# Normalizing rows ahead of an MLP and splitting the last output sums: a polynomial attention and Fourier mixing kernel on one core

## The chip, the cores and the metric

The kernel runs on one core of one Trainium2 chip. The metric is the device time of one execution in microseconds (us). A core has five engines with a queue of instructions each: TensorE (PE, matrix products; PEld are its weight loads), VectorE (DVE), ScalarE (ACT), GpSimd (POOL) and SyncE (SP, which here issues transfers). They run side by side and wait for each other by semaphores. TensorE writes its products to PSUM, which has 8 banks of 512 f32 columns by 128 partitions; the other data stands in SBUF.

## The reference: what is computed

Four batches, 4 heads, 1088 tokens, head size 32. First an attention with polynomial features, without softmax:

```
a, b  = S1 x, S2 x                     (8 values each per token, for q and k)
phi   = outer(a, b)                    (64 features)
kv    = sum over tokens of phi(k) v    z = sum over tokens of phi(k)
x     = (phi(q) kv) / (phi(q) z + 1e-6)          -> [batch, 1088, 128]
```

Then a mixing layer and an MLP:

```
u   = x + real(FFT over tokens and over the 128 features of x)
un  = (u - mean(u)) / sqrt(var(u) + 1e-6)        (per token)
out = u + relu(un @ w1) @ w2                     (128 -> 512 -> 128)
```

## The kernel before, in words

The whole order is written out by hand in one table (lines 28 to 79). A word such as `UB,A,-1,0,2` names a step, the engine that carries it out (P, V, A, G for POOL, S), the PSUM bank (or -1) and the step's arguments, mostly batch and group. Each engine carries out its own words in the table's order; the framework adds the waits. In what follows a step is named with its arguments: UB 0,2 is batch 0, group 2.

The 1088 tokens of a batch are cut into groups 0 and 1 of 512 (four blocks of 128) and group 2 of 64. For each batch:

- **Attention.** LQ, LK, LV load. QT, KT transpose on VectorE. QA, QB (lines 394 and 398) project q into PSUM, QE copies one factor out, and QM (VectorE, line 414) or QF and QG (ScalarE and POOL, lines 420 and 424) multiply the two. KP, KE and KM (POOL, line 365) do the same for k, KV (line 371) sums over tokens, KZ (line 389) copies kv and z out. ND and NN (lines 429 and 436) are the denominator and the numerator; DT, DE, RC, BT make the reciprocals, XM (line 466) gives x in bf16.
- **Mixing.** FD (line 478) is the transform over features, PE (line 490) copies it out, TD (line 496) is the transform over tokens, TE and CX (lines 513 and 516) copy it out. AN and XN make reversed copies for group 1.
- **u and its statistics, batches 0 to 2.** UU (line 584) makes rows of u in PSUM, token by token, US (line 593) copies them to SBUF in f32, UB (line 531) casts them to bf16, TP (line 542) transposes them with TensorE, UE (line 549) copies the transposed block out. BS (line 535) takes the row statistics, SD (line 573) the square root of the variance for all nine blocks of a batch at once, RS (line 581) its reciprocal.
- **u, batch 3.** UT (line 520) makes u transposed and centred straight away, UQ squares it, VR sums the squares, VT transposes the sums, and then come SD and RS. UU and US follow late, for the output sum alone.
- **MLP.** w1 is centred over its rows ahead of time (CM, CE), so that u need not be. M1 (line 599) multiplies by w1, RL (line 614) applies the relu, M2 (line 625) multiplies by w2. A factor 1/std per token passes through relu and both products, so the kernel multiplies by it only at the end.
- **Output.** For batches 0, 2 and 3, FS (line 659, instructions of line 664) computes product times 1/std plus u, in blocks of 128 columns on VectorE. For batch 1, groups 0 and 1, FM (line 642) multiplies on VectorE and FA (line 653) adds on POOL. ST (line 669) stores a group in two halves (rho 0 and 1), from SP but for three of batch 3's stores, which ScalarE's queue issues. The output tile `ot` has one buffer for group 0 and one for group 1, so a batch's sums wait for the stores of the batch before.

Buffers that differ by batch (us, ub, uT, X, AB, rs, sd) are taken in turns of two; hT, the relu's output, in turns of three.

Of the kernel before, what the change touches and what calls it, by code (L numbers as in the profile page):

```python
# [28 lines left out]
INIT0,V,-1 LS,A,-1,1 INIT,G,-1 LQ,S,-1,0,0 LS,S,-1,0 SX,V,-1 QT,V,-1,0,0 LQ,S,-1,0,1 QT,V,-1,0,2 LK,S,-1,0,0
QT,V,-1,0,1 LK,S,-1,0,1 LQ,S,-1,1,1 KT,V,-1,0,0 SQ,A,-1 SA,A,-1,1 INI2,G,-1 SA,G,-1,0 SC,G,-1 WARM,P,0,0 WARM,P,1,1  # L30
WARM,P,2,2 WARM,P,3,3 WARM,P,4,4 WARM,P,5,5 WARM,P,6,6 WARM,P,7,7 QA,P,0,0,0 QE,A,-1,0,0,1 QE,A,-1,0,0,0 QB,P,4,0,0
QA,P,0,0,1 QM,V,-1,0,0,1 KT,V,-1,0,1 QF,A,-1,0,0,0 KP,P,4,0 QE,A,-1,0,1,0 QE,A,-1,0,1,1 QT,V,-1,1,1 QA,P,0,1,1
QE,A,-1,1,1,0 KE,V,-1,0 QB,P,4,0,1 LV,S,-1,0,0 SB,S,-1,1 LQ,S,-1,1,0 SB,S,-1,2 LV,S,-1,0,1 QE,A,-1,1,1,1 QT,V,-1,1,0
QT,V,-1,1,2 QA,P,0,1,0 VP,A,-1,0 QM,V,-1,0,1,0 QM,V,-1,0,1,1 QG,G,-1,0,0,0 KM,G,-1,0,0 SB,S,-1,3 LK,S,-1,1,1
KT,V,-1,1,1 KV,P,4,0,0 KM,G,-1,0,1 SB,S,-1,4 LK,S,-1,1,0 QE,A,-1,1,0,1 QE,A,-1,1,0,0 QB,P,0,1,0 KT,V,-1,1,0 KP,P,5,1
QF,A,-1,1,0,0 QF,A,-1,1,0,1 KV,P,-1,0,1 KE,V,-1,1 KZ,A,-1,0,2 KZ,A,-1,0,1 QB,P,0,1,1 SB,S,-1,5 LK,S,-1,2,0 KT,V,-1,2,0
SB,S,-1,6 LV,S,-1,1,1 KZ,A,-1,0,0 KZ,A,-1,0,3 SB,S,-1,7 LK,S,-1,2,1 KM,G,-1,1,0 KM,G,-1,1,1 ND,P,7,0,0 QM,V,-1,1,1,1
SB,S,-1,8 LV,S,-1,1,0 KT,V,-1,2,1 ND,P,4,0,1 DT,V,-1,0,0 VP,A,-1,1 KW,P,5,1,0 DE,V,-1,0,0 DT,V,-1,0,1 QM,V,-1,1,1,0
SB,S,-1,9 LB,S,-1 SB,S,-1,10 LK,S,-1,3,1 SB,S,-1,11 LQ,S,-1,2,1 QG,G,-1,1,0,1 NN,P,1,0,1 SB,S,-1,12 LQ,S,-1,2,0
DE,A,-1,0,1 RC,V,-1,0,1 RC,V,-1,0,0 SB,S,-1,13 LV,S,-1,2,1 KP,P,6,2 QG,G,-1,1,0,0 BT,V,-1,0,1 KW,P,-1,1,1 QT,V,-1,2,0  # L40
QT,V,-1,2,2 XM,V,-1,0,1 QB,P,0,2,0 KE,V,-1,2 NN,P,6,0,0 SB,S,-1,14 LK,S,-1,3,0 SB,S,-1,15 LC,S,-1,2 SB,S,-1,16
LV,S,-1,2,0 KZ,A,-1,1,0 KZ,A,-1,1,3 KZ,A,-1,1,1 KZ,A,-1,1,2 ND,P,5,1,0 SB,S,-1,17 LC,S,-1,0 SB,S,-1,18 LQ,S,-1,3,0
SB,S,-1,19 LC,S,-1,1 SB,S,-1,20 LW,S,-1,2 SB,S,-1,21 LQ,S,-1,3,1 QT,V,-1,2,1 BT,V,-1,0,0 QF,A,-1,2,0,1 ND,P,4,1,1
XM,V,-1,0,0 QF,A,-1,2,0,0 QA,P,0,2,1 DT,V,-1,1,0 FD,P,6,0 KM,G,-1,2,0 DT,V,-1,1,1 QE,A,-1,2,1,0 QE,A,-1,2,1,1
NN,P,4,1,0 DE,A,-1,1,1 PE,A,-1,0,1 PE,A,-1,0,0 DE,V,-1,1,0 RC,V,-1,1,0 KT,V,-1,3,1 QA,P,0,2,0 QE,A,-1,2,0,1
QE,A,-1,2,0,0 BT,V,-1,1,0 TD,P,6,0 TE,A,-1,0 CX,A,-1,0,0 VP,G,-1,2 XM,V,-1,1,0 RC,V,-1,1,1 KM,G,-1,2,1 KT,V,-1,3,0
NN,P,4,1,1 CX,A,-1,0,2 CW,A,-1,2 CX,A,-1,0,1 BT,V,-1,1,1 CX,V,-1,0,3 KP,P,2,3 XM,V,-1,1,1 KV,P,0,2,0 XN,G,-1,0
QG,G,-1,2,0,1 QB,P,4,2,1 KE,V,-1,3 FD,P,2,1 UU,P,1,0,0 SB,S,-1,22 LV,S,-1,3,1 QF,A,-1,2,1,1 AN,A,-1,0 QG,G,-1,2,0,0
SB,S,-1,23 LW,S,-1,1 SB,S,-1,24 LV,S,-1,3,0 PE,A,-1,1,1 VP,G,-1,3 QT,V,-1,3,0 QT,V,-1,3,2 QM,V,-1,2,1,0 PE,V,-1,1,0
QA,P,4,3,0 UU,P,2,0,1 KV,P,-1,2,1 US,V,-1,0,1 US,A,-1,0,0 QG,G,-1,2,1,1 UB,G,-1,0,1 KM,G,-1,3,0 QE,A,-1,3,0,1  # L50
QE,A,-1,3,0,0 QT,V,-1,3,1 BS,V,-1,0,0 KZ,V,-1,2,0 CW,A,-1,1 KZ,V,-1,2,2 QB,P,4,3,0 UU,P,3,0,2 QF,A,-1,3,0,1
US,A,-1,0,2 XN,A,-1,1 TD,P,1,1 TE,A,-1,1 CX,A,-1,1,2 CX,A,-1,1,0 CX,A,-1,1,3 KZ,V,-1,2,1 KZ,V,-1,2,3 QG,G,-1,3,0,1
KM,G,-1,3,1 ND,P,0,2,0 QM,V,-1,3,0,0 BS,V,-1,0,1 CX,V,-1,1,1 UB,A,-1,0,0 UB,A,-1,0,2 ND,P,3,2,1 DT,V,-1,2,0
DE,A,-1,2,0 DT,V,-1,2,1 QA,P,4,3,1 CM,P,1 CE,V,-1 DE,A,-1,2,1 RC,V,-1,2,1 RC,V,-1,2,0 UU,P,2,1,2 QE,A,-1,3,1,0
QE,A,-1,3,1,1 TP,P,0,0,0 KV,P,3,3,0 TP,P,1,0,1 UE,A,-1,0,1 UE,A,-1,0,0 BT,V,-1,2,1 US,V,-1,1,2 UB,G,-1,1,2 AN,G,-1,1
NN,P,4,2,1 NN,P,6,2,0 UU,P,2,1,0 M1,P,0,0,1,1 BT,V,-1,2,0 BS,V,-1,0,2 XM,V,-1,2,0 XM,V,-1,2,1 KV,P,-1,3,1 QB,P,4,3,1
US,V,-1,1,0 UB,G,-1,1,0 SD,A,-1,0 RL,A,-1,0,1,1 QF,A,-1,3,1,1 FD,P,0,2 QM,V,-1,3,1,0 TP,P,2,1,2 UU,P,4,1,1
M1,P,5,0,0,0 PE,A,-1,2,0 BS,V,-1,1,0 PE,V,-1,2,1 US,V,-1,1,1 BS,V,-1,1,2 RS,V,-1,0 KZ,A,-1,3,3 UE,A,-1,1,2 KZ,A,-1,3,2
KZ,A,-1,3,0 KZ,A,-1,3,1 TP,P,7,1,0 RL,A,-1,0,0,0 M1,P,0,0,0,1 QG,G,-1,3,1,1 UB,G,-1,1,1 XN,G,-1,2 RL,A,-1,0,0,1
UE,V,-1,1,0 BS,V,-1,1,1 TD,P,2,2 TP,P,4,0,2 M1,P,6,1,0,0 UE,A,-1,0,2 M1,P,0,0,1,0 M1,P,4,0,2,0 M2,P,5,0,0 TE,V,-1,2  # L60
RL,V,-1,0,2,0 RL,A,-1,1,0,0 CX,A,-1,2,1 RL,A,-1,0,1,0 FS,V,-1,0,0,0 TP,P,4,1,1 UE,A,-1,1,1 CX,V,-1,2,0 ND,P,6,3,0
ND,P,7,3,1 CX,A,-1,2,3 DT,V,-1,3,0 DT,V,-1,3,1 ST,S,-1,0,0,0 M1,P,0,1,0,1 DE,A,-1,3,0 FS,V,-1,0,0,1 SD,A,-1,1
M1,P,4,1,2,0 M2,P,6,0,2 DE,A,-1,3,1 RS,V,-1,1 RC,V,-1,3,1 CX,A,-1,2,2 FS,V,-1,0,2,0 M2,P,7,0,1 M1,P,2,1,1,0
RL,A,-1,1,0,1 RL,A,-1,1,2,0 RC,V,-1,3,0 FS,V,-1,0,1,0 FS,V,-1,0,1,1 BT,V,-1,3,0 RL,A,-1,1,1,0 UU,P,5,2,0 M1,P,0,1,1,1
AN,G,-1,2 US,A,-1,2,0 UB,A,-1,2,0 ST,S,-1,0,0,1 BT,V,-1,3,1 M2,P,6,1,0 NN,P,2,3,0 NN,P,4,3,1 RL,A,-1,1,1,1 FM,V,-1,1,0
UU,P,7,2,1 FA,G,-1,1,0 XM,V,-1,3,0 M2,P,0,1,1 XM,V,-1,3,1 US,A,-1,2,1 UB,A,-1,2,1 TP,P,6,2,0 FD,P,3,3 BS,V,-1,2,1
UU,P,1,2,2 UE,A,-1,2,0 FM,V,-1,1,1 ST,S,-1,0,2,0 M2,P,2,1,2 ST,S,-1,0,1,0 ST,S,-1,0,1,1 US,V,-1,2,2 BS,V,-1,2,0
PE,A,-1,3,0 PE,A,-1,3,1 M1,P,5,2,0,0 TP,P,7,2,1 RL,V,-1,2,0,0 FA,G,-1,1,1 UB,G,-1,2,2 M1,P,0,2,0,1 UE,A,-1,2,1
RL,A,-1,2,0,1 TD,P,3,3 TE,A,-1,3 CX,A,-1,3,1 ST,S,-1,1,0,0 CX,A,-1,3,2 ST,S,-1,1,0,1 CX,A,-1,3,3 TP,P,7,2,2
M1,P,5,2,1,0 M1,P,0,2,1,1 UE,V,-1,2,2 FS,V,-1,1,2,0 BS,V,-1,2,2 SD,A,-1,2 M2,P,7,2,0 ST,S,-1,1,1,1 ST,S,-1,1,1,0  # L70
RL,A,-1,2,1,0 CX,V,-1,3,0 UT,P,3,3,2 UT,P,2,3,1 UE,A,-1,3,1 UT,P,4,3,0 RL,V,-1,2,1,1 M1,P,6,2,2,0 M2,P,5,2,1
UE,A,-1,3,0 M1,P,0,3,0,1 UQ,A,-1,3,2 RL,A,-1,2,2,0 ST,S,-1,1,2,0 UQ,A,-1,3,1 UQ,A,-1,3,0 RS,V,-1,2 FS,V,-1,2,0,0
FS,V,-1,2,0,1 ST,S,-1,2,0,0 FS,V,-1,2,1,0 UE,V,-1,3,2 M1,P,6,3,0,0 UU,P,2,3,0 FS,V,-1,2,1,1 M2,P,3,2,2 US,V,-1,3,0
RL,A,-1,3,0,1 VR,P,4,3 M1,P,0,3,1,1 RL,A,-1,3,0,0 FS,V,-1,2,2,0 M1,P,2,3,1,0 M2,P,6,3,0 ST,S,-1,2,0,1 ST,S,-1,2,1,0
AN,G,-1,3 XN,G,-1,3 UU,P,5,3,1 M1,P,7,3,2,0 VT,V,-1,3 SD,A,-1,3 RL,A,-1,3,1,0 RL,V,-1,3,1,1 M2,P,2,3,1 ST,S,-1,2,1,1
ST,S,-1,2,2,1 US,A,-1,3,1 RL,A,-1,3,2,0 UU,P,4,3,2 ST,S,-1,2,2,0 RS,V,-1,3 FS,V,-1,3,0,0 FS,V,-1,3,0,1 M2,P,5,3,2
FS,V,-1,3,1,0 ST,S,-1,3,0,0 US,A,-1,3,2 ST,A,-1,3,0,1 ST,S,-1,3,1,0 FS,V,-1,3,2,0 FS,V,-1,3,1,1 ST,A,-1,3,2,0
ST,A,-1,3,2,1 ST,S,-1,3,1,1
"""


# [60 lines left out]
class Steps:  # L142
# [389 lines left out]
        n, m, c = (128, 4, 4 * g) if g < 2 else (64, 1, 8)  # L532
        self.copy(e, self.ub[b % 2][0:n, c : c + m, :], self.us[b % 2][0:n, c : c + m, :])

    def BS(self, e, bk, b, g):
# [4 lines left out]
        self.whole.add(b)  # L540
# [81 lines left out]
        else:  # L622
            self.nc.vector.tensor_scalar(out=out, in0=in_, scalar1=0.0, scalar2=None, op0=MAX)

    def M2(self, e, bk, b, g):
# [30 lines left out]
        self.eng(e).tensor_tensor(out=self._oo(b, g), in0=_ap(self.tm[g], 0, n, 0, dims),  # L656
                                  in1=_ap(self.us[b % 2], 0, n, 512 * g, dims), op=ADD)

    def FS(self, e, bk, b, g, rho):
        n = 128 if g < 2 else 64  # L660
        for f in range(2 if g < 2 else 1):
            i = 2 * f + rho
            o = 0 if g == 2 else 256 * rho + 128 * (1 - f if g == 0 else f)
            self.nc.vector.scalar_tensor_tensor(  # L664
                out=self.o2[b % 2][:, :] if g == 2 else self.ot[g][:, o : o + 128], in0=self.bank(("m2", b, g), 0, n, 128 * i, [[1, 128]]),
                scalar=self.rs[b % 2][0:n, 4 * g + i : 4 * g + i + 1], in1=self.us[b % 2][0:n, 4 * g + i, :],
                op0=MULT, op1=ADD)
# [61 lines left out]
```

## Time and profile before

| what | value |
|---|---|
| median of three executions | 81.86 us (81.79 to 82.59) |
| profiled execution | 81.78 us, span 79.9 us |
| TensorE busy | 69.3 us (87% of the span) |
| VectorE busy | 61.4 us (77%) |
| ScalarE busy | 55.0 us (69%) |
| GpSimd busy | 42.2 us (53%) |
| chain that ended last | PE 53%, ACT 22%, DVE 7%, DMA 5% |
| last matrix product starts | 74.43 us and just after (4 weight loads, M2 3,2) |
| last output sum ends | 75.89 us |

The span runs from the first to the last instruction that the profiler saw. Matrix products are pipelined: each is shown with its latency (0.22 us for 128 columns in bf16), while the next starts 0.055 us later, so a step's length on TensorE is read from one step's start to the next one's. The profile's groups give the count of a kind of instruction, its busy time and the mean of one; the chain follows from the last instruction back to what released it.

### The profile page before, as it was taken

The page shows a single profiled execution, that of the slowest core. Times are in us where ns is not written, and L with a number is a line of the kernel's source. Part 1 is how long each engine was busy: PE and PEld are TensorE (multiplying, and loading weights), DVE is VectorE, ACT ScalarE, POOL GpSimd, SP SyncE. Part 2 cuts the span into 40 slices and gives each one's busy share as a digit, 9 for nine tenths or more (in the row PEclk, how much of TensorE's full clock was granted, in tenths as well). Part 3 has the DMA queues.
Part 4 walks back from the last instruction along what each step waited for, and adds up shares of the span by engine and source line. Part 5 has one row for each costly group of instructions (what it writes and reads, how often), then busy time and mean ns, then how long its engine had stood idle before and what let it go on. Part 6 is the DMA issues. An engine that isn't in the chain of part 4 may idle for free.

```text
span 79.9 us, 3447 instructions
## 1 busy us (share of the span) xinstructions
PE 69.3 (87%) x1457; PEld 41.4 (52%) x1462; DVE 61.4 (77%) x144; ACT 55.0 (69%) x114; POOL 42.2 (53%) x60
## 2 busy tenths in 40 slices
PE   3949799798899999799999999999999998999400
...
DVE  1055757949999996978999989769998868899800
ACT  2412657859209579487999669998998789997300
POOL 6840338939999999995999167101142705000000
...
GB/s 24 188 315 369 278 335 285 259 245 325 288 285 300 309 232 231 12 0 8 4 8 0 8 0 8 0 0 66 83 143 41 91 131 25 36 187 57 66 211 6
DMA packets 8659, 10.90 MB, mean 136 GB/s; under 512 B 1092, under 2 KB 5956, under 8 KB 8644
## 3 DMA queue, kind: packets, MB, share of 16 engines
...
## 4 chain that ended last, share of the span: by engine, by line
PE 53%; ACT 22%; DVE 7%; DMA 5%; issue 4%; POOL 3%; SPq 1%; DVEq 0%; ACTq 0%
PE banks L235 53%; ACT hT L621 10%; DMA qin<-in_q_dram 5%; ACT aS L222 4%; POOL kp L367 3%; ACT AB L222 2%; DVE ot L664 1%; ACT us L222 1%; ACT vpad L222 1%; DVE ab L363 1%; DVE qp L416 1%; DVE X L469 1%; SPq L232 1%; ACT hE L621 1%; DVE kT L343 1%
## 5 line engine op out<-in xcount | busy, mean ns | idle before, releaser
L367 POOL TENSOR_TENSOR kp<-ab 128x1152 f32<-128x1152 f32 x8 | 17.3, 2173 | 3.1 <-DVE ab L363 3.1
L222 ACT COPY aS<-banks 128x576 f32<-128x576 f32 (+1 forms) x16 | 9.0, 616 | 6.8 <-PE banks L235 6.7
L621 ACT ACTIVATE hT<-banks 128x1024 bf16<-128x1024 f32 x13 | 13.2, 1039 | 0.5 <-PE banks L235 0.4
L426 POOL TENSOR_TENSOR qp<-bS,aS 128x576 f32<-128x576 f32 (+1 forms) x8 | 10.9, 1376 | 4.6 <-ACT bS L222 4.6
L235 PE MATMUL banks<-qp,kvz 64*32 64x256 f32 (+3 forms) x192 | 9.7, 398 | 0.4 <-ACT kvz L222 0.3
L235 PE MATMUL banks<-uT,w1c 128*128 128x512 bf16 (+1 forms) x44 | 9.1, 312 | 0.4
L235 PE MATMUL banks<-w2b,hT 128*128 128x128 bf16 x128 | 8.5, 219 | 0.1
L235 PEld LDWEIGHTS banks<-vpad,kp 128*32 128x32 f32 (+1 forms) x504 | 6.6, 113 | 3.6 <-POOL kp L367 2.4
L235 PE MATMUL banks<-qT,sab 32*64 32x288 f32 x128 | 7.1, 501 | 1.5 <-DVE qT L348 1.3
L664 DVE SCALAR_TENSOR_TENSOR ot<-banks,rs,us 128x128 f32<-128x128 f32 x24 | 7.0, 342 | 1.5 <-PE banks L235 0.7
L235 PEld LDWEIGHTS <-hT 128*128 128x128 bf16 x128 | 7.5, 98 | 1.1 <-ACT hT L621 0.4
L235 PE MATMUL banks<-vpad,kp 128*32 128x34 f32 (+1 forms) x504 | 7.5, 202 | 0.7 <-ACT vpad L222 0.3
L235 PE MATMUL banks<-qU,sab 32*64 32x256 f32 x128 | 6.8, 496 | 0.9 <-DVE X L469 0.6
L416 DVE TENSOR_TENSOR qp<-banks,aS 128x512 f32<-128x512 f32 (+1 forms) x8 | 5.5, 697 | 2.4 <-PE banks L235 2.3
L235 PE MATMUL banks<-cb,X 128*128 128x256 bf16 (+1 forms) x56 | 7.2, 250 | 0.0
L222 ACT COPY bS<-banks 128x576 f32<-128x576 f32 (+1 forms) x8 | 4.8, 630 | 3.0 <-PE banks L235 1.9
L235 PEld LDWEIGHTS <-X 128*128 128x128 bf16 x56 | 5.2, 98 | 2.6 <-issue 1.7
L226 POOL COPY ABn<-AB 128x512 bf16<-128x512 bf16 x3 | 1.8, 610 | 8.5 <-ACT AB L222 8.5
L538 DVE BATCH_NORM_STATS2 st<-us 128x6 f32<-128x256 f32 (+1 forms) x15 | 5.7, 410 | 0.1
L469 DVE TENSOR_TENSOR X<-banks,rb 128x512 bf16<-128x512 f32 (+1 forms) x8 | 5.5, 714 | 0.2
L464 DVE STREAM_TRANSPOSE rb<-rc 128x512 f32<-128x512 f32 (+1 forms) x8 | 5.6, 716 | 0.0
L343 DVE STREAM_TRANSPOSE kT<-kin 128x544 f32<-128x544 f32 x8 | 5.6, 712 | 0.0
...
## 6 DMA issues: line engine op xcount, KB each, us to landing
...
```

The costliest lines, as they stand in the source:

```text
L222: self.nc.scalar.copy(out, in_)
L226: self.nc.gpsimd.tensor_copy(out, in_)
L235: self.nc.tensor.matmul(out, l, r, start=start, stop=stop)
L343: self.nc.vector.transpose(self.kT[b % 2][:, 576 * i : 576 * i + 544], self.kin[b % 2][:, 544 * i : 544 * i + 544])
L367: self.eng(e).tensor_tensor(out=_ap(self.kp[b % 2], 0, 128, 1152 * p, [[64, 18], [8, 8], [1, 8]]), in0=_ap(a, 0, 128, 288 * p, [[16, 18], ...
L416: self.nc.vector.tensor_tensor(out=self.qp[b % 2][:, 2 * u : 2 * u + 2, o : o + n], in0=self.bank(("qb", b, r), off=1024 * u, dims=[[512, ...
L426: self.eng(e).tensor_tensor(out=self.qp[b % 2][:, 2 * u : 2 * u + 2, o : o + n], in0=self.bS[u][:, :, 0:n], in1=self.aS[b % 2][:, 2 * u : ...
L464: self.nc.vector.transpose(self.rb[r][:, :, 0 : 32 * n], _ap(self.rc[r], 0, 128, 0, [[1, 2], [2, n], [0, 32]]))
L469: self.nc.vector.tensor_tensor(out=out, in0=self.bank(("nn", b, r), dims=[[512, 2], [1, n]]), in1=self.rb[r][:, :, 0:n], op=MULT)
L538: self.nc.vector.bn_stats(self.st[b % 2][0:n, 2 * g + i, :], _ap(self.us[b % 2], 0, n, 512 * g + 256 * i, [[1, 128], [128 if g < 2 else 0, ...
L621: self.nc.scalar.activation(out=out, in_=in_, func=ACT.Relu)
L664: self.nc.vector.scalar_tensor_tensor(out=self.o2[b % 2][:, :] if g == 2 else self.ot[g][:, o : o + 128], in0=self.bank(("m2", b, g), 0, n ...
```

## The change

Five edits:

1. **UN takes the place of UB** in batches 0 to 2. It multiplies u by 1/std while it casts to bf16: on ScalarE one activation per block of 128 columns, with the block's column of `rs` as its scale; on POOL one product with `rs` broadcast along the columns. TP now comes after BS, SD and RS of its batch.
2. **FU takes the place of FS, FM and FA** in batches 0 to 2: one VectorE instruction per group, product plus u, without 1/std.
3. **Batch 3 keeps FS's formula** but for groups 0 and 1 it is cut into single blocks: FV on VectorE (product times 1/std plus u), or FT on ScalarE (times 1/std, PSUM to SBUF) followed by FC on POOL (plus u). Three of the eight blocks go by FT and FC.
4. **M2 of batch 3**, groups 0 and 1, is cut into two parts (blocks 0 and 2, blocks 1 and 3), each a step.
5. **The table is reordered** from about half of it on. The words at its start stand in another sequence, but each engine's own order is the same in the first part: on TensorE up to ND 2,0, on VectorE up to QM 3,0,0, on ScalarE up to TE 1, on POOL up to QG 2,1,1, on SP up to ST 0,0,1.

The core of the diff:

```diff
+    def UN(self, e, bk, b, g):
+        n, m, c = (128, 4, 4 * g) if g < 2 else (64, 1, 8)
+        if e == "A":
+            for i in range(c, c + m):
+                self.nc.scalar.activation(out=self.ub[b % 2][0:n, i, :], in_=self.us[b % 2][0:n, i, :], func=ACT.Copy,
+                                          scale=self.rs[b % 2][0:n, i : i + 1])
+        else:
+            self.eng(e).tensor_tensor(out=self.ub[b % 2][0:n, c : c + m, :], in0=self.us[b % 2][0:n, c : c + m, :],
+                                      in1=_ap(self.rs[b % 2], 0, n, c, [[1, m], [0, 128]]), op=MULT)
...
-    def M2(self, e, bk, b, g):
-        self.bk["m2", b, g] = bk
+    def M2(self, e, bk, b, g, part=-1):
+        if part <= 0:
+            self.bk["m2", b, g] = bk
...
         for i in range(4):
+            if part >= 0 and i % 2 != part:
+                continue
...
+    def FU(self, e, bk, b, g):
+        n = 128 if g < 2 else 64
+        dims = [[256, 2], [128, 2], [1, 128]] if g < 2 else [[1, 128]]
+        self.nc.vector.tensor_tensor(out=self._oo(b, g), in0=self.bank(("m2", b, g), 0, n, 0, dims),
+                                     in1=_ap(self.us[b % 2], 0, n, 512 * g, dims), op=ADD)
...
+    def FT(self, e, bk, b, g, i):
+        self.nc.scalar.activation(out=self.tm[g][:, 128 * i : 128 * i + 128],
+                                  in_=self.bank(("m2", b, g), 0, 128, 128 * i, [[1, 128]]), func=ACT.Copy,
+                                  scale=self.rs[b % 2][:, 4 * g + i : 4 * g + i + 1])
+
+    def FC(self, e, bk, b, g, i):
+        o = self._oc(g, i)
+        self.eng(e).tensor_tensor(out=self.ot[g][:, o : o + 128], in0=self.tm[g][:, 128 * i : 128 * i + 128],
+                                  in1=self.us[b % 2][:, 4 * g + i, :], op=ADD)
```

FV is one FS instruction for a block that is named; `_oc` gives its column in `ot`.

Each engine's order after the part that is kept, with the steps' arguments (the number behind @ is a bank):

```
TensorE after: QA 3,1 @4  ND 2,1 @3  KV 3,0 @1  UU 1,2 @2  CM @0  QB 3,1 @4  TP 0,0 @2  UU 1,1 @3  UU 1,0 @0  TP 0,1 @6
 M1 0,0,1 @4  NN 2,0 @2  NN 2,1 @6  KV 3,1  M1 0,1,0 @4  TP 0,2 @0  FD 2 @6  M1 0,1,1 @2  M1 0,0,0 @4  ND 3,0 @1  ND 3,1 @0
 TD 2 @2  NN 3,0 @6  NN 3,1 @4  TP 1,0 @0  M2 0,0 @1  M1 0,2,0 @6  M2 0,1 @7  TP 1,1 @0  UU 2,0 @2  M2 0,2 @6  UU 2,1 @4
 M1 1,0,0 @0  UU 2,2 @3  M1 1,0,1 @6  FD 3 @4  M1 1,1,0 @2  M1 1,1,1 @0  M2 1,0 @6  TD 3 @4  TP 2,0 @2  M2 1,1 @3  TP 2,1 @0
 TP 1,2 @7  M1 2,0,0 @1  TP 2,2 @6  M1 2,0,1 @4  UT 3,1 @3  M1 2,1,1 @6  UT 3,0 @0  M1 2,1,0 @1  M2 2,0 @4  M1 1,2,0 @5
 M1 3,0,1 @6  UT 3,2 @3  M2 2,1 @1  M1 3,0,0 @4  VR 3 @0  M2 1,2 @1  M1 3,1,0 @6  M1 2,2,0 @2  M1 3,1,1 @4  M2 3,0 part 0 @0
 M2 2,2 @2  UU 3,0 @3  M2 3,0 part 1  UU 3,1 @6  M2 3,1 part 0 @2  M1 3,2,0 @1  M2 3,1 part 1  UU 3,2 @7  M2 3,2 @1
VectorE, the end: FU 2,1  VT 3  FU 1,2  RL 2,2,0  AN 3  RS 3  FU 2,2  US 3,0  FV 3,0,2  FV 3,0,0  FV 3,1,2  FV 3,1,3  FV 3,1,1  FS 3,2,0
ScalarE, the end: RL 3,0,0  SD 3  RL 3,1,0  RL 3,1,1  FT 3,0,3  FT 3,0,1  US 3,1  FT 3,1,0  RL 3,2,0  ST 3,0,1  US 3,2  ST 3,1,0  ST 3,2,0
POOL after: KM 3,0  QG 3,0,1  AN 1  UN 0,2  UN 0,1  KM 3,1  QG 3,1,0  XN 2  UN 1,0  UN 1,1  AN 2  UN 2,0  UN 2,2  XN 3
 FC 3,0,3  FC 3,0,1  FC 3,1,0
SP, the end: ST 2,0,0  ST 2,0,1  ST 2,1,0  ST 2,1,1  ST 1,2,0  ST 2,2,1  ST 2,2,0  ST 3,0,0  ST 3,1,1  ST 3,2,1
```

UN 0,0, UN 1,2 and UN 2,1 are ScalarE's.

More of the change, by code (lines that the diff above doesn't have):

```diff
@@ L28 @@
 TABLE = """
[L29 to L78, printed above, removed]
+INIT0,V,-1 INIT,G,-1 LS,A,-1,1 LQ,S,-1,0,0 LS,S,-1,0 SQ,A,-1 LQ,S,-1,0,1 INI2,G,-1 LK,S,-1,0,0 LK,S,-1,0,1 LQ,S,-1,1,1
@@ new lines @@
+LV,S,-1,0,0 SX,V,-1 QT,V,-1,0,0 SA,A,-1,1 SA,G,-1,0 SC,G,-1 QT,V,-1,0,2 SB,S,-1,1 LQ,S,-1,1,0 QT,V,-1,0,1 WARM,P,0,0
+WARM,P,1,1 WARM,P,2,2 WARM,P,3,3 WARM,P,4,4 WARM,P,5,5 WARM,P,6,6 WARM,P,7,7 QA,P,0,0,0 QB,P,4,0,0 KT,V,-1,0,0
+QE,A,-1,0,0,1 SB,S,-1,2 LV,S,-1,0,1 QE,A,-1,0,0,0 QM,V,-1,0,0,1 QF,A,-1,0,0,0 QA,P,0,0,1 SB,S,-1,3 LK,S,-1,1,1
+KT,V,-1,0,1 QG,G,-1,0,0,0 QT,V,-1,1,1 SB,S,-1,4 LK,S,-1,1,0 QE,A,-1,0,1,0 KP,P,4,0 QE,A,-1,0,1,1 SB,S,-1,5 LK,S,-1,2,0
+KE,V,-1,0 QA,P,0,1,1 QT,V,-1,1,0 SB,S,-1,6 LV,S,-1,1,1 QE,A,-1,1,1,0 QB,P,4,0,1 KM,G,-1,0,0 QE,A,-1,1,1,1 QT,V,-1,1,2
@@ new lines @@
+QM,V,-1,0,1,0 SB,S,-1,7 LK,S,-1,2,1 VP,A,-1,0 QA,P,0,1,0 QM,V,-1,0,1,1 SB,S,-1,8 LV,S,-1,1,0 QE,A,-1,1,0,1 KT,V,-1,1,1
+KM,G,-1,0,1 QE,A,-1,1,0,0 KV,P,4,0,0 KT,V,-1,1,0 SB,S,-1,9 LB,S,-1 QB,P,0,1,0 SB,S,-1,10 LK,S,-1,3,1 KP,P,5,1
+QF,A,-1,1,0,0 SB,S,-1,11 LQ,S,-1,2,1 QF,A,-1,1,0,1 KV,P,-1,0,1 KE,V,-1,1 SB,S,-1,12 LQ,S,-1,2,0 KT,V,-1,2,0
+KM,G,-1,1,0 QB,P,0,1,1 KZ,A,-1,0,2 KZ,A,-1,0,1 KZ,A,-1,0,0 KZ,A,-1,0,3 SB,S,-1,13 LV,S,-1,2,1 VP,A,-1,1 QM,V,-1,1,1,1
+ND,P,7,0,0 KT,V,-1,2,1 ND,P,4,0,1 SB,S,-1,14 LK,S,-1,3,0 DT,V,-1,0,0 KM,G,-1,1,1 KW,P,5,1,0 DE,V,-1,0,0 SB,S,-1,15
@@ new lines @@
+LC,S,-1,2 DT,V,-1,0,1 QM,V,-1,1,1,0 DE,A,-1,0,1 SB,S,-1,16 LV,S,-1,2,0 RC,V,-1,0,1 RC,V,-1,0,0 NN,P,1,0,1 BT,V,-1,0,1
+SB,S,-1,17 LC,S,-1,0 KP,P,6,2 QG,G,-1,1,0,1 QT,V,-1,2,0 KW,P,-1,1,1 SB,S,-1,18 LQ,S,-1,3,0 QT,V,-1,2,2 XM,V,-1,0,1
+QG,G,-1,1,0,0 KE,V,-1,2 SB,S,-1,19 LC,S,-1,1 QB,P,0,2,0 KZ,A,-1,1,0 QT,V,-1,2,1 KZ,A,-1,1,3 KZ,A,-1,1,1 KZ,A,-1,1,2
+SB,S,-1,20 LW,S,-1,2 NN,P,6,0,0 QF,A,-1,2,0,1 BT,V,-1,0,0 KM,G,-1,2,0 QF,A,-1,2,0,0 ND,P,5,1,0 SB,S,-1,21 LQ,S,-1,3,1
+XM,V,-1,0,0 ND,P,4,1,1 DT,V,-1,1,0 QA,P,0,2,1 SB,S,-1,22 LV,S,-1,3,1 DT,V,-1,1,1 DE,V,-1,1,0 FD,P,6,0 QE,A,-1,2,1,0
```

57 lines of the change are left out of this document (48 added, 9 removed).

## The prediction

> **What bounds the kernel now.** First the page's 40 slices (2.0 us each; PEclk is 9 in all but the last, so no price needs a clock correction):
>
> ```profile
> PE   3949799798899999799999999999999998999400
> DVE  1055757949999996978999989769998868899800
> ACT  2412657859209579487999669998998789997300
> POOL 6840338939999999995999167101142705000000
> ```
>
> To see: from 48 us on TensorE and ScalarE are both full; POOL has room. Then the chain that ended last, in order of time (start, length, what):
>
> ```profile
> 49.25 1.94 ACT hT L621 x2
> ...
> 58.79 1.02 ACT hT L621
> ...
> 59.86 2.76 PE banks L235 x36
> 62.62 0.05 issue
> 62.67 3.98 PE banks L235 x51
> 66.65 1.01 ACT hT L621
> 67.67 0.04 issue
> 67.71 5.72 PE banks L235 x72
> ...
> 74.52 0.35 DVE ot L664
> ...
> 75.37 0.52 DVE ot L664 x2
> ```
>
> To see: ScalarE's evictions lead to 59.8, TensorE from there to 73.4, VectorE's output sums at the end (done 75.89). The last store is issued by 76.46; 3.4 us later the span ends. Third, the groups by shape (count, busy us, mean ns), for prices:
>
> ```profile
> L621 ACT ACTIVATE hT<-banks 128x1024 bf16<-128x1024 f32 x13 | 13.2, 1039 | 0.5 <-PE banks L235 0.4
> L656 POOL TENSOR_TENSOR ot<-tm,us 128x512 f32<-128x512 f32 x2 | 2.5, 1268 | 4.4 <-DVE tm L645 4.4
> L222 ACT CAST ub<-us 128x512 bf16<-128x512 f32 x3 | 1.9, 619 | 0.1
> L222 ACT CAST ub<-us 64x128 bf16<-64x128 f32 x1 | 0.3, 293 | 0.0
> L454 ACT ACTIVATE de<-dT,eps 128x18 f32<-128x18 f32 x2 | 0.6, 323 | 0.2 <-DVE dT L448 0.2
> ```
>
> **The change part by part.** Steps carry the table's names, a number being batch and group. The profiled execution took 81.78 us (span 79.9, 1.9 around it), the median of three is 81.86; I sum against 81.78.
>
> *TensorE's work stays.* The orders part at 39.72 us. From there the same steps remain, by their start-to-start times in the timeline: 8 full M2 x 0.89, 16 full M1 x 0.43, 6 full UU x 0.47, 6 full TP x 0.22, 2 FD x 0.96, 2 TD x 1.16, 4 NN x 0.54, 3 ND x 0.52, 2 KV x 0.76, QA and QB 1.28, UT 0.92, VR 0.62, CM 0.21, and the small groups of M2, M1, UU, TP 1.83: 32.5 us. The last M2 ends its issue at 74.65, so 74.65 - 39.72 - 32.5 = 2.4 us of gaps are in it today. The change can take from TensorE only those, and from the tail (74.65 to 76.46) some of 1.8.
>
> *UB becomes UN (batches 0 to 2).* On ScalarE one 0.62 cast becomes four pieces of 128 columns with a scale read per row. No row shows this. Low end: the casts of 128 columns (0.29; start to start 0.20, if they overlap by 0.1 as two hT do, 1.94 for two): 0.9 for four. High end: no overlap at all, 0.45 from start to start: 1.8. Nearest are the ScalarE rows that read an operand per row: de, 0.32 for 18 columns. From the 512-column copy (0.585) to hT's median of 1.02 at 1024 is 0.85 ns a column, so 128 columns cost 0.32 + 0.09 = 0.41, and 0.31 start to start: 1.34 for four, which I take: 0.7 more than a cast, for UN 0,0 and for UN 2,1; the 64-row UN 1,2 costs 0.41 for 0.29. The Trainium skill (ScalarE: Activation LUTs, section What ACT_TABLE_LOAD costs) states that a pointer operand per row adds about 93 ns and that neighbours overlap by as much; four pieces are then an estimated 1.27, and the sum would be about 0.1 lower. That rule stands on the side of the de row, against the cheap casts, and so against the change; no run yet shows a scale operand.
>
> On POOL a 0.61 cast becomes a product of two f32 operands: 1.27 (the ot row, same 512 columns), bounds 0.61 and 2.17 (kp, 1152 columns with broadcasts). Five large ones and two small, covered as named below.
>
> *The wait for 1/std.* Today TP needs only us; now TP waits for BS of all three groups, SD (0.30), RS (0.20), UN. Batch 0: TE 1 and four CX end on ScalarE at 41.0, QE 3,1,0 and SD 0 at 41.8, RS 0 at 42.0; UN 0,0 runs 42.2 to 43.55. TP 0,0 starts at 43.6 instead of 41.45. Ahead of it TensorE now has QA 3,1, ND, KV, UU 1,2, CM and QB 3,1, to 42.95: it idles 0.65. Behind RS 0 on VectorE wait DT 2,1, RC, US, DE, CE (0.45 idle; CE ends 43.4, ahead of the first M1 at 45.0). Behind UN 0,0 on ScalarE wait QF 3,1,0 and UE 0,0. On POOL KM 3,0 moves up 1.5; UN 0,2 and 0,1 (42.1 to 43.6) hold KM 3,1 till 45.75, KV 3,1 needs it only at 46.6. If POOL took 2.17, 0.1 late. Batch 1: RS 1 ends at 51.2, UN 1,0 at 52.5; TP 1,0 is due at 53.1 behind batch 3's ND, TD 2 and NN, which moved forward and are the cover; without them TP would wait the whole 1.3 of UN. Batch 2: RS 2 at 59.8, UN 2,0 done 61.1, TP 2,0 due 61.45 behind TD 3; at 2.17 it would be 0.5 late.
>
> *Sums.* FS of batches 0 and 2 (1.05 for four blocks) becomes one FU each, priced as tm (0.66; bounds 0.6 start to start and 0.68, qp from PSUM): 4 x 0.45 = 1.8 off VectorE. For batch 1, FM and FA (0.66 + 1.27) become FU (0.66): off POOL. VectorE idles at RS 0, RS 2 (0.9) and elsewhere in the new order, so this is no time by itself. PE 2,0 (0.59), two KZ (0.21 each) and a DE go from ScalarE to VectorE and pay part of UN's 1.4.
>
> *ScalarE from US 2,1 (56.85) to the last RL*, start to start: 9 RL x 0.92, SD 0.54, PE 0.49, UN 1.24, TE and three CX 1.5, UE 1.5, UQ 1.07, US 1.0, three FT 0.95 (bounds 0.27 and 0.45 each), small RL 0.3: 16.9. With 0.3 of waiting for VT at SD 3 (RL 3,1,0 stands behind it) and 0.2 of small waits it ends at 74.3: as full as TensorE.
>
> *Gaps of the new TensorE order*, so followed: 0.2 (QA 3,1 until QM 3,0,0 ends 39.88), 0.15 (QB behind QE 3,1,1), 0.65 (TP 0,0), 0.3 for three changes from bf16 to f32 (0.1 as at 57.94 to 58.03), 0.3 (M1 2,0,1 for CX 3,3's bank), 0.15 (M2 2,1 for RL 2,1,0), 0.1 (VR), 0.1 in bank waits, 0.4 (last M2 for RL 3,2,0): 2.35. So the last M2 ends at 39.72 + 32.5 + 2.35 = 74.6: nothing gained.
>
> *Tail.* Today the last M2 is followed by FS 3,2,0, then two blocks of FS 3,1,1 (to 75.89), then their store. After, FT and FC take three of eight blocks to ScalarE and POOL (FC 0.45: between a 0.28 cast and 1.27 for 512 columns), and FV 3,1,1 comes ahead of FS 3,2,0: M2 74.6, FS 3,2,0 from 74.85 (0.27 after, as M2 to FS at 52.67 to 52.94) to 75.2, stores of the small group issued by 75.8 on SP and ScalarE's queue, each behind one other (0.55). ST 3,0,1 on ScalarE stands ahead of US 3,2 and waits for FC 3,0,1 at 73.8: issued to 74.45, US 3,2 to 74.75, in time. SP's stores of batch 2 and ST 1,2,0 are issued by 73.1; ot is free again (2.3 from issue to landing, 1.6 or more spare). Gain 76.46 - 75.8 = 0.65.
>
> Sum: 81.78 + 0 (TensorE) - 0.65 (tail) = 81.1.
>
> **Rivals.** *Cheap pieces: 80.1.* If UN and FT go at the casts' 0.20, TP 0,0 starts 0.4 earlier, and ScalarE's last stretch is 0.44 (UN 2,1) + 0.33 (FT) shorter; the gaps that ScalarE makes (0.65, 0.3, 0.15, 0.4) shrink by 1.0 in all: 81.1 - 1.0. For it: casts and squares of this size overlap (sq 64 columns to the next: 0.11). Against: the de and sd rows (0.32, 0.30).
>
> *Pieces without overlap: slower, 82.4.* The place is the same. At 0.45 start to start, eight UN pieces and three FT add 11 x 0.14 = 1.5, of which some 1.3 reaches the last M2, as both engines are full: 81.1 + 1.3. It turns slower than before above 0.31 + 0.65 / 11 = 0.37. For it: the kvz copies stand 0.22 apart at 0.21 each, with no overlap; against: sq, hT and uT overlap by 0.1 to 0.15.
>
> *The store in ScalarE's queue: slower, 82.7.* ST 3,0,1 waits for two FC on POOL and holds US 3,2. An FC at 0.45 hides it; every 0.1 more on FC delays the end by 0.2, so above 0.78 it is slower than before, and at 1.27 it would be 1.6 later than forecast: 82.7. Against: qp's 512 to 576 columns (1.27 to 1.41) give 2.2 ns a column, so 0.43 for 128.
>
> *Hidden: 81.7.* If the 0.65 at TP 0,0 comes on top of today's 2.4 us of gaps instead of in place of some of them, it eats the tail's gain. For it: both engines are full after 48 us, so a late start may not be made up; against: batch 3's attention steps fill TensorE meanwhile.
>
> **How the numbers follow.** Forecast (80.7 to 81.5, 81.1): 0.45. Cheap pieces: 0.22. No overlap, or hidden (81.5 to 82.5): 0.22. Store in the queue, or another stall that large: 0.11. One per cent is about what a measurement can tell from no change: 81.04 and 82.68. Faster is the cheap case and somewhat under half of the forecast's: 0.42. Slower is the last case and the top of the third: 0.14. Same: 0.44. The range leaves out a tenth on each side: 80.1 to 82.6.
>
> **What would show it.** Right: the first part equal to 39.7; TP 0,0 about 2.1 later, with its wait on ScalarE's ub; X of batch 3 done near 55.8 instead of 60.3; ub pieces at 0.41; POOL's ub at 1.27; the last M2 within 0.5 of 74.6; last store issued 0.65 earlier. Wrong: ub pieces under 0.3 or not overlapping, TP 1 or TP 2 waiting for POOL, ScalarE idle after 60 us, or US 3,2 late behind the store.

## The result, and the profile after

The changed kernel takes 86.38 us (median of 4 executions, 86.32 to 86.50), the kernel before 81.94 us beside it on the same chip (4 executions, 81.79 to 82.59). The ratio is 1.058, 95% interval 1.051 to 1.065: slower by 4.4 us, outside the predicted 80.1 to 82.6. No rival had this place or this size. In the experiments executions of one kernel spread by 2 us and more; medians are of all executions, ratios and intervals of those within 1.5% of the kernel's fastest.

The kept part is equal: the first QM 3,0,0 starts on VectorE at 39.28 (39.12 before). The span is 84.5 (79.9). The 40 slices of the changed kernel, 2.1 us each:

```profile
PE   4907899789999999999990499999999999999710
DVE  1036867579999989779799967998996859667530
ACT  3314639585145895889993081788999999989800
POOL 6830639749999999997399200226202700000600
PEclk9997556999999999999999957999999999999995
```

To see: the 22nd and 23rd slice (44.4 to 48.6) are a hole in TensorE (0, 4), while VectorE is busy (9, 9), and the granted clock is 0.5 and 0.7 behind it. The low clock in the 4th to 7th slice is from before QM 3,0,0 and changed little: that step starts 0.16 later. The chain that ended last, in the stretch where it differs (start, length, what):

```profile
42.83 0.50 DVE de L456
43.33 3.68 issue
47.01 0.68 DVE w1c L307
47.73 21.18 PE banks L235 x346
...
```

To see: no ScalarE evictions between 49 and 60 any more. The chain stands in one VectorE instruction, a DE, and in 3.68 us behind it in which the profile shows no releaser; CE (w1c) follows, and then TensorE has no long wait until 69. VectorE's and POOL's instructions in that stretch (start, length, engine, line, operation; two timelines):

```profile
42.61 0.22 DVE L224 COPY us<-banks 64x128 f32<-64x128 f32 x1
42.75 4.33 DVE L456 TENSOR_SCALAR de<-dT 128x16 f32<-128x16 f32 x1
47.01 0.67 DVE L307 TENSOR_TENSOR w1c<-w1f,banks 128x512 bf16<-128x512 f32 x1
```

```profile
42.32 1.39 POOL L542 TENSOR_TENSOR ub<-us,rs 64x128 bf16<-64x128 f32 x2 [0.47 <-DVE rs L592]
43.67 2.16 POOL L367 TENSOR_TENSOR kp<-ab 128x1152 f32<-128x1152 f32 x1
45.80 1.26 POOL L426 TENSOR_TENSOR qp<-bS,aS 128x512 f32<-128x512 f32 x1
```

To see: DE 2,1, 16 columns, lasts 4.33 us and ends at 47.08. POOL has work without a gap from 42.32 (the two UN, KM 3,1, QG 3,1,0) and ends at 47.06. Behind the DE waits CE; UU 1,0 may not write bank 0 before CE has read it, and TensorE stands until 47.73. The waits of TensorE from 39 to 84 us (what, total, times, longest) and the stretches (length; busy us of PE, PEld, DVE, ACT, POOL; clock; DMA share; GB/s) say the rest:

```profile
PE banks L235 <- DVE w1c L307: 3.4, 1, 3.4
PE banks L235 <- ACT hE L631: 0.6, 1, 0.6
```

```profile
44.40:47.70 3.30, 0.00 (x0) 0.00 (x0) 3.30 (x3) 0.68 (x2) 2.65 (x2) 1.00 0.00 0
47.70:52.50 4.80, 4.77 (x119) 2.45 (x119) 3.50 (x7) 2.00 (x3) 0.00 (x0) 0.64 0.02 3
```

One wait of 3.4 us, and 4.8 us at a granted clock of 0.64 behind it. Last, the groups by shape (count, busy us, mean ns) for the new operations:

```profile
L542 POOL TENSOR_TENSOR ub<-us,rs 128x512 bf16<-128x512 f32 x4 | 4.1, 1038 | 7.0 <-DVE rs L592 7.0
L539 ACT ACTIVATE ub<-us,rs 128x128 bf16<-128x128 f32 x8 | 2.6, 413 | 0.0
L704 POOL TENSOR_TENSOR ot<-tm,us 128x128 f32<-128x128 f32 x3 | 1.3, 456 | 12.0 <-ACT tm L698 12.0
```

Four UN pieces on ScalarE take 1.28 to 1.30 (1.34 taken), FC 0.46 (0.45), UN on POOL 1.04 (1.27). These prices were near or too high; what was lost stands elsewhere. The estimate of 1.27 for the four pieces from the Trainium skill (ScalarE: Activation LUTs, section What ACT_TABLE_LOAD costs) agrees with the 1.28 to 1.30.

### The profile page after: what moved, and what is told of

Read it like the earlier page. It is cut to its first block, busy times and chain, and to the rows that moved or that the text cites. A ratio compares the mean times of both kernels' runs of the same rounds, so it can differ in the third digit from the quotient of the medians.

```text
span 84.5 us, 3443 instructions
## 1 busy us (share of the span) xinstructions
PE 71.1 (84%) x1462; PEld 41.9 (50%) x1462; DVE 63.1 (75%) x134; ACT 56.0 (66%) x118; POOL 43.0 (51%) x61
## 4 chain that ended last, share of the span: by engine, by line
PE 66%; issue 7%; ACT 7%; DVE 6%; DMA 5%; POOL 3%; SPq 1%; ACTq 1%
PE banks L235 66%; DMA qin<-in_q_dram 5%; ACT aS L222 4%; POOL kp L367 3%; ACT AB L222 2%; DVE ab L363 1%; DVE X L469 1%; DVE ot L675 1%; SPq L232 1%; DVE w1c L307 1%; ACTq L232 1%; ACT Xn L222 1%; DVE de L456 1%; SPq L268 0%; DVE qT L348 0%
## 5 line engine op out<-in xcount | busy, mean ns | idle before, releaser
L235 PE MATMUL banks<-qp,kvz 64*32 64x256 f32 (+3 forms) x192 | 10.8, 443 | 0.3 <-ACT kvz L222 0.2
L235 PE MATMUL banks<-uT,w1c 128*128 128x512 bf16 (+1 forms) x48 | 10.3, 328 | 0.0
L542 POOL TENSOR_TENSOR ub<-us,rs 128x512 bf16<-128x512 f32 (+1 forms) x6 | 4.8, 823 | 7.5 <-DVE rs L592 7.5
L235 PE MATMUL banks<-qU,sab 32*64 32x256 f32 x128 | 7.3, 495 | 0.6 <-ACT aS L222 0.5
L704 POOL TENSOR_TENSOR ot<-tm,us 128x128 f32<-128x128 f32 x3 | 1.3, 456 | 12.0 <-ACT tm L698 12.0
L222 ACT CAST uT<-banks 128x512 bf16<-128x512 f32 (+1 forms) x8 | 4.4, 550 | 4.2 <-PE banks L235 4.1
L222 ACT CAST AB<-banks 1x144 bf16<-1x144 f32 (+1 forms) x18 | 6.3, 352 | 0.9 <-PE banks L235 0.5
L235 PEld LDWEIGHTS banks<-qp,kvz 64*32 64x32 f32 (+1 forms) x192 | 3.6, 115 | 5.4 <-issue 1.9
```

What stands on the lines that cost most here:

```text
L222: self.nc.scalar.copy(out, in_)
L235: self.nc.tensor.matmul(out, l, r, start=start, stop=stop)
L542: self.eng(e).tensor_tensor(out=self.ub[b % 2][0:n, c : c + m, :], in0=self.us[b % 2][0:n, c : c + m, :], in1=_ap(self.rs[b % 2], 0, n, c, ...
L704: self.eng(e).tensor_tensor(out=self.ot[g][:, o : o + 128], in0=self.tm[g][:, 128 * i : 128 * i + 128], in1=self.us[b % 2][:, 4 * g + i, : ...
```

## The experiments

Theory: a DE of 16 columns on VectorE is held for as long as POOL works, and the hole and the clock behind it are the whole loss. Rivals: CE or the new wait for 1/std is late by itself; the loss is the new order as such; VectorE beside POOL is slow whatever the shape.

Start-up ahead of QM 3,0,0 differs between executions (it starts between 37.9 and 42.7 us in the profiles here), so profiles are compared from its start. "Sums" is the end of the last output sum, "issue" that of the last store's issue, "end" that of the span, each in us behind the start of QM 3,0,0; each row is one profile.

| kernel | sums | issue | end | median, executions |
|---|---|---|---|---|
| before | 36.77 | 37.34 | 40.74 | 81.6 to 82.0 by chip |
| changed | 41.69 | 42.64 | 45.26 | 86.38, 4 |
| e1: DE 2,1 on ScalarE | 36.45 | 37.42 | 40.01 | 81.14, 6 |
| e2: before, DE 2,1 on VectorE | | 38.38 | 41.85 | 82.91, 4 |
| e3: changed, gap filled | | 41.10 | 43.70 | 84.41, 4 |
| e4: DE 2,1 of nine blocks | 36.45 | 37.41 | 40.01 | 80.74, 12 |
| e4b: e4 again | 36.45 | 37.42 | 40.04 | 80.64, 12 |
| e5: e4, sums whole | 36.59 | 37.56 | 40.21 | 80.65, 12 |
| e7: changed, gap in POOL's order | 37.63 | 38.59 | 41.20 | 83.63, 2 |
| e8: e4, own bank | 35.92 | 37.05 | 39.76 | 80.85, 6 |
| e12: e8 again | 35.95 | 37.08 | 39.79 | 80.87, 12 |
| e9: e4, UN without 1/std | 35.78 | 36.75 | 39.35 | 80.19, 12 |
| e10: before, small store last | 36.77 | 37.87 | 40.60 | 81.70, 6 |
| e11: e8, one small store | 35.93 | 36.61 | 40.43 | 81.40, 12 |

**e1: the DE back on ScalarE.**

```diff
-QF,A,-1,3,1,0 US,V,-1,1,2 TP,P,2,0,0 UE,A,-1,0,0 DE,V,-1,2,1 CE,V,-1
+DE,A,-1,2,1 QF,A,-1,3,1,0 US,V,-1,1,2 TP,P,2,0,0 UE,A,-1,0,0 CE,V,-1
```

> The changed kernel with one step moved back: DE 2,1 (16 columns) on ScalarE, ahead of QF 3,1,0, as in the kernel before. Theory (VectorE's DE 2,1 needs something that GpSimd holds while its instructions follow each other without a gap, 42.3 to 47.1 us): no VectorE instruction over 1.3 us, TensorE's 3.4 us wait for w1c and the low clock behind it (0.64 from 47.7 to 52.5) are gone, UU 1,0 starts near 44.3, time 81.0 (80.5 to 81.6). Rival (CE itself was late, for an operand or for TensorE's bank, and DE only looks long): the wait for w1c stays, time within 0.5 of 86.4.

Measured: 81.14 us (79.40 to 81.48; before 81.72 on that chip). The hole is gone, CE starts at 42.80, and the end is 5.25 earlier. One word of the table is the whole loss. e1 also shows a 16-column instruction that POOL does not hold, in its two timelines:

```profile
43.73 2.17 POOL L367 TENSOR_TENSOR kp<-ab 128x1152 f32<-128x1152 f32 x1
```

```profile
44.03 0.24 DVE L460 RECIPROCAL rc<-de 128x16 f32<-128x16 f32 x1
```

RC of the same 16 columns, SBUF to SBUF, takes its 0.24 in the middle of KM.

**e2: the same word in the kernel before**, nothing else.

```diff
-DE,A,-1,2,1
+DE,V,-1,2,1
```

> The kernel before with that one step alone: DE 2,1 from ScalarE to VectorE. It comes up on VectorE near 42.2 us while GpSimd runs KM 3,1 till 43.3. Theory (held by GpSimd): the instruction lasts 1.0 to 1.2 us and ends within 0.1 of KM 3,1's end; time 81.9 to 83. Rival (the long DE belongs to the new order, not to the move): 0.14 to 0.2 us, time within 0.4 of the kernel before.

Measured: 82.91 us (82.12 to 83.25 but for one at 87.97), ratio 1.023, interval 0.982 to 1.064: unclear by time, clear by the trace, from POOL's and VectorE's timelines of e2:

```profile
41.00 2.18 POOL L367 TENSOR_TENSOR kp<-ab 128x1152 f32<-128x1152 f32 x1
```

```profile
42.12 1.09 DVE L456 TENSOR_SCALAR de<-dT 128x16 f32<-128x16 f32 x1
```

KM 3,1 ends at 43.18 and the DE at 43.21. Here POOL has a gap behind KM, so the hold is 1.1 and the end 1.1 later. It needs neither UN nor the new order.

**e3: the hole filled.** 14 products of zeros (512 columns) into a free bank, ahead of UU 1,0 on TensorE.

```diff
+WARM,P,5,0
...
 QM,V,-1,3,1,1 UU,P,0,1,0
```

> The changed kernel with 14 matrix products of 512 columns into a free bank ahead of UU 1,0, which fill some 3.0 of TensorE's 3.4 us of waiting; DE 2,1 stays as it is. Theory (part of the loss is the clock that falls after TensorE idles): DE still lasts 4.3 us and UU 1,0 still starts near 47.7, but the granted clock stays 1.0 from 47.7 to 52.5 and the time falls by 1.8 to 84.6 (84.2 to 85.0). Rival (the clock is low for another reason, or costs nothing since other engines set the pace there): time 86.0 to 86.8.

Measured: 84.41 us (83.50 to 85.09). The DE still takes 4.34, and the same stretches of e3 read

```profile
44.40:47.70 3.30, 3.28 (x19) 1.47 (x17) 3.30 (x2) 0.97 (x3) 2.96 (x2) 1.00 0.02 5
47.70:52.50 4.80, 4.46 (x127) 2.77 (x127) 4.74 (x11) 2.58 (x5) 0.61 (x1) 1.00 0.01 3
```

The clock stays at 1.0, and the end is 1.6 earlier than in the changed kernel. So of 5.2 us lost against e1, 1.6 is the clock behind the hole and 3.7 the hole. The Trainium skill (TensorE: Matmul & The Clock Gate, section What's actually happening) gives about 3.4 us of idle time as what lowers the clock; the 3.37 us without a product here are close to it.

**e4: the same DE, on VectorE, in the same place, over nine blocks instead of eight** (two columns more, of ones, that nobody reads).

```diff
-        n = 9 - r
+        n = 9 if (b, r) == (2, 1) else 9 - r
```

> The changed kernel with DE 2,1 kept on VectorE, but over nine blocks in place of eight (18 columns; the ninth is not read by anyone, and its two columns of dT are set once at the start by GpSimd). Theory A (only the even shape uses what GpSimd holds, as the 18-column DE 0,0, 1,0 and 2,0 ran in 0.14 to 0.19 us beside a busy GpSimd): 0.15 to 0.2 us, no wait for w1c, time 80.9 (80.5 to 81.6). Theory B (any such instruction is held, and the 18-column ones had luck): about 4.3 us again, time 86.4.

Measured: 80.74 us (79.98 to 81.64), ratio 0.997, interval 0.991 to 1.002; again as e4b: 80.64, ratio 1.002 (0.995 to 1.008).

> The same kernel as e4_de_nine, here as the base of the three runs beside it. Expected: 80.7 us, 0.5 to 1.2 less than the kernel before; from the first QM 3,0,0 to the end of the span 39.9 us (40.8 before).

From POOL's and VectorE's timelines of e4:

```profile
41.57 1.39 POOL L543 TENSOR_TENSOR ub<-us,rs 64x128 bf16<-64x128 f32 x2 [0.48 <-DVE rs L593]
```

```profile
42.01 0.15 DVE L457 TENSOR_SCALAR de<-dT 128x18 f32<-128x18 f32 x1
```

0.15 us, in the middle of POOL's UN: the shape decides, not the place, the buffers or the order. By the times the mended kernel and the kernel before are not told apart; by the profiles its end is 0.7 earlier.

**e7: a gap in POOL's order.** QG 3,1,0, which waits for ScalarE, ahead of KM 3,1; the DE of 16 columns stays on VectorE.

```diff
-UN 0,2  UN 0,1  KM 3,1  QG 3,1,0
+UN 0,2  UN 0,1  QG 3,1,0  KM 3,1
```

> The changed kernel with one step of POOL moved: QG 3,1,0 ahead of KM 3,1. QG waits for ScalarE's QF 3,1,0 (done at 44.1 in the changed kernel), so POOL has a gap of about 0.4 us behind UN 0,1 (43.67). Theory A (DE 2,1 of 16 columns is held until POOL pauses): DE starts at 42.75 and ends at 43.7, 0.95 long instead of 4.33; UU 1,0 about 3 us earlier; KM 3,1 then stands 1.5 later, of which KV 3,1 passes on a part: 81.5 to 83 us. Theory B (it is held for a set number of POOL instructions, or by what these instructions are): about 4 us long and 85 to 86 us.

Measured: 81.90 and 85.36 us, the first of them the profiled one. From POOL's and VectorE's timelines of e7:

```profile
41.96 1.39 POOL L541 TENSOR_TENSOR ub<-us,rs 64x128 bf16<-64x128 f32 x2 [0.47 <-DVE rs L591]
43.83 1.28 POOL L425 TENSOR_TENSOR qp<-bS,aS 128x512 f32<-128x512 f32 x1 [0.47 <-ACT bS L221]
```

```profile
42.40 0.99 DVE L455 TENSOR_SCALAR de<-dT 128x16 f32<-128x16 f32 x1
```

The second UN ends at 43.35, POOL pauses for 0.47, and the DE ends at 43.39. In the changed kernel POOL passed from one instruction to the next at 43.67 and 45.80 without letting the DE in; a pause lets it in at once. What is paid then is KM: TensorE waits 0.8 for it. Why the other execution took 85.36 is open.

**e9: what 1/std costs in the mended kernel.** UN is a plain cast in the same places (0.62 on ScalarE), so batches 0 to 2 lack the factor.

```diff
+        self.copy(e, self.ub[b % 2][0:n, c : c + m, :], self.us[b % 2][0:n, c : c + m, :])
```

> The kernel of e4, but UN is a plain cast in the same places (one instruction on ScalarE, one on POOL), without 1/std: the outputs of batches 0 to 2 lack that factor. It tells what the four pieces and the wait for 1/std still cost. By the prediction's steps TP 0,0 would start 0.6 earlier and ScalarE's last stretch be 0.7 shorter, of which some reaches the end: 0.3 to 0.8 less than e4, 80.2 us. If TensorE's work alone sets the end behind 48 us (the rival that hides it): the last M2 as in e4 but for 0.2, 80.6 us.

Measured: 80.19 us, ratio 0.987 (0.980 to 0.995); end 0.69 earlier than e4b, sums 0.67. The pieces and the wait for 1/std together cost 0.7 in the profiles, 0.45 in the medians.

**e5, e10: the tail.** e5 is e4 with whole M2 3,0 and M2 3,1 and FS for all blocks, no FT, no FC; the small group's stores stay last (M1 3,2,0 goes ahead of M2 3,1 and US 3,2 ahead of ST 3,0,1 as well):

```diff
-M2 3,1 part 0  M2 3,1 part 1  FT 3,1,0  FV 3,1,2  FC 3,1,0  FV 3,1,3  FV 3,1,1  FS 3,2,0
+M2 3,1  FS 3,1,0  FS 3,1,1  FS 3,2,0
```

e10 is the kernel before with only that last order; ST 3,2,1 goes from ScalarE's queue to SP with it:

```diff
-FS 3,1,0  FS 3,2,0  FS 3,1,1  ST 3,2,0  ST 3,2,1  ST 3,1,1
+FS 3,1,0  FS 3,1,1  ST 3,1,1  FS 3,2,0  ST 3,2,0  ST 3,2,1
```

> The kernel of e4, but batch 3's sums are whole again: M2 3,0 and M2 3,1 in one step each, FS for all eight blocks on VectorE, no FT and no FC; the small group's sum and its stores stay last. Theory A (the cut into single blocks is worth the 0.65 us of the prediction's tail): last store issued 0.5 to 0.7 later than in e4, 81.4 us. Theory B (in e4 the FV of a group start only behind its FT, so the cut saves VectorE three blocks and costs it a wait of the same length, and the gain at the end is that the last store is the 16 KB one): last store issued within 0.2 of e4's, 80.7 us.

> The kernel before, with nothing but the order of its last steps changed: FS 3,1,1 ahead of FS 3,2,0, and the two 16 KB stores of the small group last. In e4 the last store is issued no earlier than before (37.4 against 37.3 us behind the first QM 3,0,0), but the span ends 2.55 behind it instead of 3.44. Theory A (the whole gain of the new tail is that a small store is last): the span ends 39.9 to 40.2 behind QM 3,0,0 (40.8 before), 81.1 us. Theory B (FT and FC are needed for it): 40.7, 81.8 us.

Measured: e5 80.65 us, ratio 0.996 (0.988 to 1.004), issue 0.14 and end 0.17 later than e4b: theory B; the cut is worth 0.1 to 0.2, not 0.65. e10: 81.70 us, ratio 0.989 (0.980 to 0.999), but in its profile the end is only 0.14 earlier than in the kernel before, so theory A isn't borne out; nor is theory B, since e5 has no FT and no FC and ends 0.4 before e10. The end comes 2.74 behind the last issue instead of 3.41, but that issue is 0.53 later: SP issues three large stores until 75.09, and the small one, ready at 74.62, from 75.21. In e4 and e5 ScalarE's queue has one of these (ST 3,1,0). Which part of the 0.4 between e10 and e5 is the queue and which the rest of the order stays open.

**e8, e12: a bank of its own.** In e4b the first FV of group 1 starts only when ScalarE's FT of the same bank has ended (0.59 idle, put down to tm). In e8 M2 3,1's second half goes to a free bank, FT takes block 1 for block 0, RL 3,2,0 and US 3,2 go ahead of what they waited behind, and ST 3,1,0 and ST 3,1,1 change queues.

```diff
-FT 3,1,0  RL 3,2,0  ST 3,0,1  US 3,2
+RL 3,2,0  FT 3,1,1  US 3,2  ST 3,0,1
```

> The kernel of e4, but the second half of M2 3,1 has a PSUM bank of its own, FT takes block 1 instead of block 0, and RL 3,2,0 comes ahead of it on ScalarE. If FV stand behind FT because both read one bank, the first two FV of group 1 now start before that FT and the last sum ends 0.4 earlier (0.35 at the last store, of which six are issued by two queues): 80.4 us. If the issue of the stores sets the end alone: as e4, 80.7.

> The kernel of e8 once more, since its interval reached nearly to 1 and the kernels before and after it in the study spread by 2 to 3 us on their chips. Expected by the spans from QM 3,0,0 (39.8 against 40.8 for the kernel before): 1.0 us less than the kernel before, ratio 0.987. If that gain were chance: 1.0 within 0.005.

Measured: 80.85 us, ratio 0.987 (0.974 to 0.999), and again 80.87, ratio 0.988 (0.982 to 0.993). VectorE's timelines of e4b, then of e8:

```profile
74.72 0.87 DVE L690 SCALAR_TENSOR_TENSOR ot<-banks,rs,us 128x128 f32<-128x128 f32 x3 [0.59 <-ACT tm L699]
```

```profile
73.32 1.55 DVE L694 SCALAR_TENSOR_TENSOR ot<-banks,rs,us 128x128 f32<-128x128 f32 x5 [0.41 <-ACT tm L703]
```

The 0.59 is gone, the five FV run as one block, and the sums end 0.5 earlier. Bank, block and order changed together, so what the bank alone gives isn't shown. With six stores on two queues, 0.37 of the 0.5 is left at the issue and 0.3 at the end. This version is below both kernels, the kernel before by 1.2%.

**e11: one small store.** The small group's two stores of 16 KB become one of 32 KB from SP.

```diff
-ST,S,-1,3,2,1 ST,A,-1,3,2,0
+ST,S,-1,3,2,0
```

> The kernel of e8, with the small group's last two stores (16 KB each, one from SP and one, issued last, from ScalarE's queue) made one of 32 KB from SP. In e8 ScalarE's store is issued at 76.24 and SP's at 75.83. Expected: the last issue 0.4 earlier than e8's and 0.6 to 1.0 earlier than e4's, the span ends 39.3 to 39.6 behind QM 3,0,0 (39.8 in e8, 40.0 in e4): 80.3 us. If one store of 32 KB lands later than two of 16 KB by as much: 39.8, 80.7 us.

Measured: 81.40 us, ratio 0.995 (0.991 to 0.999). The last issue is 0.44 earlier than in e8, as expected, but the end is 0.67 later: 3.83 behind the issue, against 2.71. The larger store's landing took back more than the issue gave, in one profile.

## Why the prediction was wrong

- **The step that failed** is a term put at nothing, in the part on sums: "PE 2,0 (0.59), two KZ (0.21 each) and a DE go from ScalarE to VectorE and pay part of UN's 1.4". The DE has no price there, and "CE ends 43.4" leaves it an estimated 0.1 to 0.2: in e1, where VectorE has no DE 2,1, CE ends 4.14 behind QM 3,0,0, which would be 43.26. VectorE's DE in the kernel before do take 0.16, but they have 18 columns; every DE of 16 columns was ScalarE's (groups by shape of the kernel before: count, busy us, mean ns):

```profile
L456 DVE TENSOR_SCALAR de<-dT 128x18 f32<-128x18 f32 x2 | 0.3, 162 | 0.0
L454 ACT ACTIVATE de<-dT,eps 128x16 f32<-128x16 f32 x4 | 1.3, 322 | 0.9 <-DVE dT L448 0.9
```

No row had this shape on VectorE, and no bounds were set. DE 2,1 took 4.33 there (e1 takes it away, e4 changes only the shape). Three DE moved, not one; the other two have 18 columns and take 0.18 and 0.19.
- **The wait list was right, its worst case was not priced.** "Behind RS 0 on VectorE wait DT 2,1, RC, US, DE, CE" is the queue in which it happened, and the first M1 was seen to have 1.6 us behind CE. But UU 1,0 needs CE too, through bank 0, and with it all of TensorE: "CE ends 43.4" became 47.68.
- **"No price needs a clock correction"** held for the profile of before and not for a kernel with 3.4 us of idle TensorE: 1.6 us more (e3).
- **The rest of the walk nearly stood.** TP 0,0 was put at 43.6, behind the whole UN 0,0; in e8, whose QM 3,0,0 starts within 0.1 of before's, its four products start one by one as the pieces end, from 43.04 to 43.60. UN in pieces lets TP begin half a us early, which the walk did not use. The last M2 was put 0.05 earlier than before; in e4b it starts 35.62 behind QM 3,0,0, against 35.31, so the gaps are 0.36 more than the 2.35 summed; its wait for RL 3,2,0 is 0.62 where 0.4 was taken.
- **The net gain came out by luck.** In e4b the end is 0.71 earlier than before, near the 0.65 forecast for the tail, but by other terms: the last M2 starts 0.31 later, from there to the last issue 0.23 is gained instead of 0.65, and from the issue to the end 0.79 (2.61 against 3.41), which the prediction held constant at 3.4. The cut into blocks, which it credited, gives 0.14 to 0.17 (e5); FV stands behind FT for 0.59 (e4b).
- **Slips that entered no total.** "Five large ones" of UN on POOL are four (the x4 row above). "4 x 0.45" takes FU at 0.60; with the 0.66 named beside it, it is 1.6 and not 1.8.
- **Rivals.** Pieces without overlap: no, four take 1.3. The store in ScalarE's queue: no, FC is 0.46. Cheap pieces: not the case, and worth less than the 1.0 given (e9, which drops the wait for 1/std as well, gains 0.7). Hidden: perhaps in part, in the 0.36 above; no run separates it. With the DE mended the kernel takes 80.6 to 81.1 us, near the forecast 81.1: without that one instruction's hold the total would have been right, though not all of its terms.
